# Rows of the scratch list in DRAM: from 1040 bytes to 1088 bytes, and clears in pieces of three rows

## The chip, the cores and the metric

The kernel runs on one core of a Trainium2 chip. The metric is the time of one execution on the device in microseconds (us). Three runs of the kernel before took 1323.39, 1324.07 and 1330.32 us; the median is 1324.07 us. The inputs are four pairs of batches (8 x 1856 tokens of 256 numbers), weights of a spectral layer, and the weights of 16 experts.

## The reference, cut to what matters

Two layers, one behind the other. The first is a transform along the sequence, a complex linear map with a soft threshold, and the transform back:

```
X = rfft(x, axis=1);  Xr, Xi = X.real, X.imag
Yr = Xr @ w_r - Xi @ w_i + b_r;   Yi = Xr @ w_i + Xi @ w_r + b_i
Yr, Yi = soft(Yr, 0.01), soft(Yi, 0.01)          # sign(v) * max(|v| - 0.01, 0)
y = irfft(Yr + 1j * Yi, n=1856, axis=1)
```

The second is a mixture of experts over the 14848 tokens of y. Each token picks one of 4 groups and in it one of 4 experts, by the largest of 4 logits each time:

```
g = argmax(y @ w_group);  e = argmax(y @ w_expert[g])
out = p_g * p_e * (relu(y @ w1[g, e]) @ w2[g, e])  # p_g, p_e: softmax values of the picks
```

## The kernel before, in words

**Stages.** The batches go through in four pairs. For a pair, x is loaded, a short transform (letters a to d of the order below) turns it, 15 steps k do the complex map (e to o), a second transform goes back (p to s) and a third one gives the token rows (t to w), which lie in a tile `vs[pr]` of 128 partitions x 32 rows x 260 numbers (RW = 260: 256 values, the token's number and its gate weight; 1040 bytes). The rows are transposed for the logits (x to z, G, H), and 'R' (route_g, about 30 short VectorE steps for 16 rows) works out to which slot of which expert's list each row goes.

**The list in DRAM.** xs_d has a stretch of CAP rows for each of the 16 experts and 128 rows behind them. Two kinds of work write it. The clears (letter 'Z', line 395, ScalarE's DMA queue, called ACTq in the profile) put zeros into the first NZ = 1152 slots of each expert, 16 transfers and one more (line 393) for the last 128 rows. The scatters ('S', line 272, GpSimd, called POOL) send 128 rows each to their slots by an indirect DMA, 128 scatters in all, 32 for a pair; 12 of each 128 rows have a slot out of bounds and aren't written. They have to come behind the clears. Later the lists are read back: six early blocks of 256 rows (line 777) while the last pairs are still in work, then blocks of 384 or 512 rows (line 430) and 128 or 64 rows (line 1003) for the experts' matmuls, from about 640 us on. The results go to the output by another indirect DMA on GpSimd (line 498).

**What sets the order.** TensorE (PE), ScalarE (ACT) and VectorE (DVE) run the first part in an order written out by hand: the string ORDER, a letter for each step. So a clear is an instruction of ACT that stands between its casts and activations, and what stands behind it on ACT starts when the clear has been issued. The first twelve or so clears stand in the 15 steps k of the first pair. One such step is, on PE, 8 matmuls of line 598 and 24 of line 641; on ACT a cast (607), a negation (611 and 622), two activations (648) and the copy of the bias into the next PSUM tile (627); on DVE lines 616 and 654. POOL and SP (the loads' queue) follow a scheduler. The tiles called `big` rotate through three buffers; a new one waits until the last user of the old one is done.

Of the kernel before, what the change touches and what calls it, by code (L numbers as in the profile page):

```python
# [10 lines left out]
F32 = mybir.dt.float32  # L11
F32R = mybir.dt.float32r
BF16 = mybir.dt.bfloat16
I32 = mybir.dt.int32
# [23 lines left out]
G, EG, NE, F = 4, 4, 16, 1024  # L38
# [3 lines left out]
CAP = N + EARLY  # L42
ROWS = NE * CAP + 128
RW = 260
NZ = 1152
OFF = float(1 << 20)
KF, KH = 7, 4
# [107 lines left out]
def spectral_moe(ctx: ExitStack, tc: tile.TileContext, x, wri, bri, wgate, w1, w2, cst, out):  # L155
    nc = tc.nc

    dram = ctx.enter_context(tc.tile_pool(name="dram", bufs=1, space=bass.MemoryType.DRAM))
    keep = ctx.enter_context(tc.tile_pool(name="keep", bufs=1))
    big = ctx.enter_context(tc.tile_pool(name="big", bufs=3))  # L160
    xp = ctx.enter_context(tc.tile_pool(name="xp", bufs=2))
    ix = ctx.enter_context(tc.tile_pool(name="ix", bufs=1))
    pg = ctx.enter_context(tc.tile_pool(name="pg", bufs=2, space=PSUM))
    xs_d = dram.tile([ROWS, RW], F32, name="xs_d")

    x_v = x.rearrange("pr dc p (r d) -> pr dc p r d", r=32)
    K = keep.tile([128, CK1 - CK0], F32, name="K")
# [11 lines left out]
    for n in (16,):  # L179
        t = keep.tile([128, NE, n], BF16, name=f"smask{n}")  # L180
# [32 lines left out]
    def route_g(pr, L, r0, n):  # L213
# [45 lines left out]
        sloti = rt.tile([128, 16], I32, name="sloti", bufs=3)[:, 0:n]  # L259
        nc.vector.tensor_scalar(out=sloti, in0=slot, scalar1=kc("PO"), scalar2=None, op0=ALU.add)  # L260
        for r in range(n):
            pend.append((pr, sloti[:, r:r + 1], vs[pr][:, r0 + r, :]))
        yield
        nc.vector.tensor_tensor(out=base, in0=base, in1=incf.rearrange("p (e r) -> p e r", e=NE)[:, :, n - 1], op=ALU.add)  # L264
        yield

    pend, sent_of = [], []

    def scatter(n):
        for _ in range(n):  # L270
# [30 lines left out]
    cf = fwd.enter_context(tc.tile_pool(name="cf", bufs=1))  # L301
# [84 lines left out]
    wg = ci.tile([128, 2, 32], F32, name="wg")  # L386
    nc.sync.dma_start(out=wg.rearrange("p c m -> p (c m)"), in_=wgate)
    late.close()
    zero = cf.tile([128, RW], F32, name="zero")
    nc.gpsimd.memset(zero, 0.0)  # L390

    def clear_steps():
        nc.scalar.dma_start(out=xs_d[NE * CAP:ROWS], in_=zero)
        for e in range(NE):
            nc.scalar.dma_start(out=xs_d[e * CAP:e * CAP + NZ].rearrange("(p j) w -> p j w", p=128),
                                in_=zero.unsqueeze(1).broadcast_to([128, NZ // 128, RW]))
            yield

    def raw_w(e):
# [26 lines left out]

    def fetch(pool, e, s0, n, bufs, idb):
        w = n // 128
        xg = pool.tile([128, 4, RW], F32, name="xg", bufs=bufs)
        nc.sync.dma_start(out=xg[:, 0:w], in_=xs_d[e * CAP + s0:e * CAP + s0 + n].rearrange("(p c) w -> p c w", p=128))  # L430
        return xg, ids_of(pool, xg, w, idb)

# [93 lines left out]
    wts, raws, low, units, vs, psum = {}, {}, {}, {}, {}, {}  # L526
    yp, early = [], {}
    jobs = EJOBS
# [147 lines left out]
    @steps_of(pairs, u16)  # L676
    def b_turn(pr, j):
        if j == 0:
            vs[pr] = big.tile([128, 32, RW], F32, name="big")
        nc.vector.transpose(out=vs[pr][:, :, j * 16:(j + 1) * 16].rearrange("p r d -> p d r"),  # L680
                            in_=psum.pop(("b", pr, j)).rearrange("p (k d b) -> p d k b", k=16, b=2))

# [89 lines left out]
    @steps_of(range(len(jobs)))  # L772
    def e_fetch(n):
        j, e = jobs[n]
        assert len(sent_of) >= 64 + 32 * j, "an early list is read before it is written"
        xgs[n] = xg = early["mp"].tile([128, 2, RW], F32, name="xg", bufs=len(jobs))
        nc.sync.dma_start(out=xg, in_=xs_d[e * CAP + j * LEV:e * CAP + j * LEV + LEV].rearrange("(p c) w -> p c w", p=128))

    @steps_of(range(len(jobs)))
# [217 lines left out]
    sp = (mybir.EngineType.SP,)  # L997

    def flex_rows(starts, used_k):
        xg = xq.tile([128, 1, RW], F32, name="xf", bufs=2)  # L1000
        n = 128 // len(starts)
        for i, st in enumerate(starts):
            nc.sync.dma_start(out=xg[i * n:i * n + n, 0, :], in_=xs_d[bass.ds(st, n), :])
        return xg, used_k
# [18 lines left out]

    def flex_ids(rows):
        xg, used_k = rows
        xi = xg[:, 0, :].bitcast(I32)
        nc.vector.tensor_tensor(out=xi, in0=xi, in1=used_k.broadcast_to([128, RW]), op=ALU.bitwise_and)
        return xg, ids_of(xq, xg, 1, 4)

# [174 lines left out]
```

## Time and profile before

| What | Value |
|---|---|
| Median of three runs | 1324.07 us |
| Profiled execution: its time, and its span | 1327.12 us, 1325.3 us |
| PE busy | 1215.2 us, 92% of the span |
| DVE, ACT, POOL busy | 764.1, 696.8, 253.2 us |
| Clears on ACTq: packets of that queue, MB | 19120, 19.46 |
| Scatters and output rows on POOL's queue: packets, MB | 12048, 30.67 |

How to read it: the span is from the first to the last instruction, 1.8 us less than the execution's time. Busy time is a sum over the span; whether an engine limits a stretch is read from that stretch. "issue" behind an idle time means that nothing the profile shows ended it. Issuing a DMA isn't counted as busy for ACT, but nothing behind it on ACT is dispatched before it is issued.

### The profile page before, as it was taken

The page shows a single profiled execution, that of the slowest core. Times are in us where ns is not written, and L with a number is a line of the kernel's source. Part 1 is how long each engine was busy: PE and PEld are TensorE (multiplying, and loading weights), DVE is VectorE, ACT ScalarE, POOL GpSimd, SP SyncE. Part 2 cuts the span into 40 slices and gives each one's busy share as a digit, 9 for nine tenths or more (in the row PEclk, how much of TensorE's full clock was granted, in tenths as well). Part 3 has the DMA queues.
Part 4 walks back from the last instruction along what each step waited for, and adds up shares of the span by engine and source line. Part 5 has one row for each costly group of instructions (what it writes and reads, how often), then busy time and mean ns, then how long its engine had stood idle before and what let it go on. Part 6 is the DMA issues. An engine that isn't in the chain of part 4 may idle for free.

```text
span 1325.3 us, 20451 instructions
## 1 busy us (share of the span) xinstructions
PE 1215.2 (92%) x7418; PEld 1048.9 (79%) x7418; DVE 764.1 (58%) x1706; ACT 696.8 (53%) x1564; POOL 253.2 (19%) x257
## 2 busy tenths in 40 slices
PE   9989997799569977777899999999999999999997
PEld 5978996787369846676798898798798878878886
DVE  5448865288646886644556556455547447446542
ACT  3776894579346745513245445444446345445532
POOL 0000004400440036443101111121121111111111
PEclk9999998799889997977999999999999999999999
DMA  9894103100410013414114345245344434434100
GB/s 383 211 271 105 65 12 112 59 1 33 154 56 4 18 41 121 152 60 153 41 60 151 120 146 207 100 135 220 99 141 155 182 111 155 181 105 159 49 21 29
DMA packets 50198, 151.71 MB, mean 114 GB/s; under 512 B 7205, under 2 KB 27818, under 8 KB 40112
## 3 DMA queue, kind: packets, MB, share of 16 engines
q1 hardware_dynamic: 18928, 100.25, 21.7%
q0 software_dynamic: 12048, 30.67, 6.4%
q10 hardware_dynamic: 19120, 19.46, 5.9%
q8 instruction: 59, 0.97, 0.3%
q14 instruction: 43, 0.35, 0.1%
HBM read 100.40 MB, written 52.46 MB: 115 GB/s over the span
## 4 chain that ended last, share of the span: by engine, by line
PE 79%; DVE 6%; ACT 5%; issue 4%; another core or an unknown queue 3%; ACTq 1%; DMA 1%; POOL 0%; POOLq 0%; DVEq 0%
PE ph L457 21%; PE py L511 15%; PE pw L641 10%; PE py L512 8%; PE bank L314 6%; PE pg L598 3%; PE ph L810 2%; PE bank L711 2%; PE pg L441 2%; PE ph L476 1%; PE bank L831 1%; PE bank L734 1%; PE py L1060 1%; PE ph L1043 1%
## 5 line engine op out<-in xcount | busy, mean ns | idle before, releaser
L511 PE MATMUL py<-big,hh 128*128 128x512 f32 x856 | 309.6, 401 | 0.0
L457 PE MATMUL ph<-xth,big 128*128 128x384 f32 (+1 forms) x928 | 269.0, 365 | 1.7 <-DVE yo L844 1.1
L512 PE MATMUL py<-big,hl 128*128 128x256 f32 x856 | 241.2, 282 | 0.9 <-DVE hl L463 0.9
L498 POOL DMA_INDIRECT out_dram<-yo,si x123 | 119.8, 974 | 617.8 <-DVE yo L519 539.0
L272 POOL DMA_INDIRECT xs_d<-big,sloti x128 | 130.6, 1020 | 428.7 <-DVE base L264 181.7
L463 DVE SCALAR_TENSOR_TENSOR hl<-ph,hh 128x256 fp32r<-128x256 f32 x464 | 157.2, 380 | 77.1 <-ACT hh L461 71.5
L511 PEld LDWEIGHTS py<-big,hh 128*128 128x128 f32 x856 | 161.0, 188 | 38.2 <-issue 3.2
L457 PEld LDWEIGHTS ph<-xth,big 128*128 128x128 f32 x928 | 172.7, 189 | 23.3 <-issue 1.7
L461 ACT ACTIVATE hh<-ph 128x256 fp32r<-128x256 f32 x464 | 139.1, 352 | 84.0 <-PE ph L457 80.6
L518 ACT ACTIVATE yo<-py,gate 128x256 f32<-128x256 f32 x107 | 50.7, 474 | 225.6 <-PE py L512 225.6
L457 PE MATMUL ph<-xtl,big 128*128 128x384 f32 (+1 forms) x464 | 169.2, 365 | 0.0
L512 PEld LDWEIGHTS py<-big,hl 128*128 128x128 f32 x856 | 161.0, 188 | 1.4 <-DVE hl L463 1.2
L519 DVE SCALAR_TENSOR_TENSOR yo<-py,gate,yo 128x256 f32<-128x256 f32 x107 | 51.8, 484 | 183.7 <-ACT yo L518 183.7
L641 PE MATMUL pw<-wh,xh 128*128 128x256 f32 x480 | 123.5, 295 | 1.1 <-ACT xh L611 0.8
L641 PE MATMUL pw<-wl,xh 128*128 128x256 f32 x480 | 120.4, 289 | 0.8 <-issue 0.8
L417 DVE TENSOR_TENSOR big<-xt,big 128x512 fp32r<-128x512 f32 x160 | 108.7, 679 | 0.0
L598 PE MATMUL pg<-CF,big 128*128 128x128 f32 x480 | 73.5, 299 | 32.5 <-issue 23.3
L416 ACT CAST big<-xt 128x512 fp32r<-128x512 f32 x160 | 99.6, 623 | 0.0
L598 PEld LDWEIGHTS pg<-CF,big 128*128 128x128 f32 x480 | 67.0, 209 | 40.8 <-issue 25.4
L641 PEld LDWEIGHTS pw<-wh,xh 128*128 128x128 f32 x480 | 95.1, 198 | 2.6 <-ACT xh L611 1.0
L641 PEld LDWEIGHTS pw<-wl,xh 128*128 128x128 f32 x480 | 95.1, 198 | 2.2 <-issue 1.5
L548 DVE TENSOR_TENSOR sl<-big,sh 128x512 fp32r<-128x512 f32 x128 | 83.7, 684 | 22.6 <-ACT sh L544 20.4
(208 smaller groups left out, 2054.4 us busy)
## 6 DMA issues: line engine op xcount, KB each, us to landing
xt<-in_w_dram SPq DMA_DIRECT2D x46, 1024.0 KB
xs_d<-zero ACTq DMA_DIRECT2D x16, 1170.0 KB
big<-in_w_dram SPq DMA_DIRECT2D x16, 1024.0 KB
big<-in_x_dram SPq DMA_DIRECT2D x8, 1024.0 KB
xt<-in_x_dram SPq DMA_DIRECT2D x8, 1024.0 KB
xg<-xs_d SPq DMA_DIRECT2D x13, 520.0 KB
xg<-xs_d SPq DMA_DIRECT2D x16, 390.0 KB
xs_d<-big,sloti POOLq DMA_INDIRECT x128
```

The costliest lines, as they stand in the source:

```text
L272: ins = nc.gpsimd.indirect_dma_start(out=xs_d, out_offset=bass.IndirectOffsetOnAxis(ap=sl_, axis=0), in_=row, in_offset=None, bounds_check ...
L416: nc.scalar.copy(out=wt[:, 2 * i, cs], in_=raws[i][:, cs])
L417: nc.vector.tensor_tensor(out=wt[:, 2 * i + 1, cs], in0=raws[i][:, cs], in1=wt[:, 2 * i, cs].bitcast(F32), op=ALU.subtract)
L457: nc.tensor.matmul(o[:, :n], lhsT=a_[:, ch, fs], rhs=b_[:, ch, 0:n], start=k == 0, stop=k == 5)
L461: nc.scalar.activation(out=hh[:, f, :m], in_=ov, func=AF.Relu)
L463: nc.vector.scalar_tensor_tensor(out=hl[:, f, :m], in0=ov, scalar=0.0, in1=hh[:, f, :m].bitcast(F32), op0=ALU.max, op1=ALU.subtract)
L498: ins = nc.gpsimd.indirect_dma_start(out=out, out_offset=bass.IndirectOffsetOnAxis(ap=ids.si[:, t:t + 1], axis=0), in_=ysb, in_offset=None ...
L511: nc.tensor.matmul(o, lhsT=hh[:, f, ts], rhs=w2b[:, :, f, :], start=f == 0, stop=f == 7, skip_group_check=True)
L512: nc.tensor.matmul(o[:, 0:D], lhsT=hl[:, f, ts], rhs=w2h[:, f, :], start=False, stop=f == 7, skip_group_check=True)
L548: nc.vector.tensor_tensor(out=lo, in0=src, in1=units[key].bitcast(F32), op=ALU.subtract)
L598: nc.tensor.matmul(o[:, m * 128:(m + 1) * 128], lhsT=zys[pr][:, k, ch * 128:(ch + 1) * 128, bt], rhs=T_v[:, k, :], start=True, stop=True)
L641: nc.tensor.matmul(y[:, bt * D:(bt + 1) * D], lhsT=a_[:, bt * 2 + ch, cs], rhs=w_[:, ri, ch, :], start=False, stop=fin, skip_group_check=True)
```

## The change

Rows of xs_d are 272 numbers apart and long (RP = 272, 1088 bytes) in DRAM and in the tiles into which they are read; in the tile that the scatters read, rows stay 260 numbers apart. A scatter now sends 272 numbers from the row's start, so the last 12 are the first 12 of the next row. Behind row 31 there are 12 new numbers, set to zero by a small memset on GpSimd for each pair. The zero tile is three rows wide, and a clear writes 384 pieces of three rows (3264 bytes) in place of 1152 rows of 1040.

```
+RP = 272
-    xs_d = dram.tile([ROWS, RW], F32, name="xs_d")
+    xs_d = dram.tile([ROWS, RP], F32, name="xs_d")
...
         for r in range(n):
-            pend.append((pr, sloti[:, r:r + 1], vs[pr][:, r0 + r, :]))
+            c = (r0 + r) * RW
+            pend.append((pr, sloti[:, r:r + 1], rows_of_pair[pr][:, c:c + RP]))
...
-    zero = cf.tile([128, RW], F32, name="zero")
+    zero = cf.tile([128, 3, RP], F32, name="zero")
     nc.gpsimd.memset(zero, 0.0)
...
-        nc.scalar.dma_start(out=xs_d[NE * CAP:ROWS], in_=zero)
+        nc.scalar.dma_start(out=xs_d[NE * CAP:ROWS], in_=zero[:, 0])
         for e in range(NE):
-            nc.scalar.dma_start(out=xs_d[e * CAP:e * CAP + NZ].rearrange("(p j) w -> p j w", p=128),
-                                in_=zero.unsqueeze(1).broadcast_to([128, NZ // 128, RW]))
+            nc.scalar.dma_start(out=xs_d[e * CAP:e * CAP + NZ].rearrange("(p a j) w -> p a (j w)", p=128, j=3),
+                                in_=zero.rearrange("p j w -> p (j w)").unsqueeze(1).broadcast_to([128, NZ // 384, 3 * RP]))
...
         if j == 0:
-            vs[pr] = big.tile([128, 32, RW], F32, name="big")
+            rows_of_pair[pr] = t = big.tile([128, 32 * RW + RP - RW], F32, name="big")
+            nc.gpsimd.memset(t[:, 32 * RW:], 0.0)
+            vs[pr] = t[:, 0:32 * RW].rearrange("p (r w) -> p r w", w=RW)
...
-        xgs[n] = xg = early["mp"].tile([128, 2, RW], F32, name="xg", bufs=len(jobs))
+        xgs[n] = xg = early["mp"].tile([128, 2, RP], F32, name="xg", bufs=len(jobs))
```

The tiles of lines 429 and 1000 grow from RW to RP in the same way, and line 1026 masks the first RW numbers of a row only.

On ACT, in the steps k of the first pair, the order of the program before has the first clears here:

```order
L393 DMA xs_d<-zero 128x260 [waits Pool_49]
L395 DMA xs_d<-zero 1152x1x260 x2
L648 ACTIVATE rp<-pw,nlam,CF 128x512 [waits PE_49]
L607 CAST xh<-pg 128x4x128
L611 ACTIVATE xh<-pg 128x4x64
L648 ACTIVATE rn<-pw,nlam,CF 128x512
L622 ACTIVATE xl<-xl 128x4x64 [waits DVE_49]
L627 COPY pw<-bias 128x512 [waits Activation_49]
L395 DMA xs_d<-zero 1152x1x260 [waits DMAHW6_49]
```

and now, two source lines further down:

```order
L395 DMA xs_d<-zero 128x272 [waits Pool_49]
L397 DMA xs_d<-zero 384x1x816 x2
L650 ACTIVATE rp<-pw,nlam,CF 128x512 [waits PE_49]
L609 CAST xh<-pg 128x4x128
L613 ACTIVATE xh<-pg 128x4x64
L650 ACTIVATE rn<-pw,nlam,CF 128x512
L624 ACTIVATE xl<-xl 128x4x64 [waits DVE_49]
L629 COPY pw<-bias 128x512 [waits Activation_49]
L397 DMA xs_d<-zero 384x1x816 [waits DMAHW6_49]
```

Nothing moved: the same 17 transfers stand at the same places behind the same waits, with 384 rows of 816 numbers where there were 1152 of 260.

On POOL, where the scatters of the second pair (big_2916) end and those of the third (big_4317) begin, the order of the program before is

```order
L272 DMA xs_d_72<-big_2916,sloti_4035 245888x260 [waits DMASW6_49,Activation_49]
L272 DMA xs_d_72<-big_2916,sloti_4035 245888x260 [waits DMASW7_49]
L272 DMA xs_d_72<-big_4317,sloti_5129 245888x260 [waits DMAHW4_49,DMASW0_49,DMAHW5_49,DVE_49,Activation_49]
L272 DMA xs_d_72<-big_4317,sloti_5129 245888x260 [waits DMASW1_49]
```

and now (big_2917, big_4319 and big_4918 are the rows of the second, third and fourth pair)

```order
L274 DMA xs_d_72<-big_2917,sloti_4037 245888x272 [waits DMASW6_49]
L274 DMA xs_d_72<-big_2917,sloti_4037 245888x272 [waits DMASW7_49,Pool_49]
L682 MEMSET big_4319 128x12 [waits DMASW4_49,DMASW3_49,DMASW5_49,DMASW2_49,DMASW6_49,DMASW1_49,DMASW7_49,DMASW0_49,PE_49]
L682 MEMSET big_4918 128x12 [waits DVE_49]
L274 DMA xs_d_72<-big_4319,sloti_5133 245888x272 [waits DMAHW4_49,DMAHW5_49,DVE_49,Activation_49]
L274 DMA xs_d_72<-big_4319,sloti_5133 245888x272 [waits Activation_49]
```

Two memsets stand between the scatters of the two pairs: that of the third pair, which waits for all scatters of the second to land, and that of the fourth, which waits for VectorE.

## Rows read from the trace of the kernel before

**Rows 1.** The page: busy time, TensorE's granted clock in 40 slices, the chain by engine.
```profile
PE 1215.2 (92%) x7418; PEld 1048.9 (79%) x7418; DVE 764.1 (58%) x1706; ACT 696.8 (53%) x1564; POOL 253.2 (19%) x257
...
PEclk9999998799889997977999999999999999999999
...
PE 79%; DVE 6%; ACT 5%; issue 4%; another core or an unknown queue 3%; ACTq 1%; DMA 1%; POOL 0%; POOLq 0%; DVEq 0%
```
**Rows 2.** Windows: from:to, length, busy time of each engine, granted clock, DMA.
```profile
core 0: us, PE busy (x) PEld busy (x) DVE busy (x) ACT busy (x) POOL busy (x), PEclk, DMA share, GB/s
...
40.00:49.00 9.00, 9.00 (x80) 9.00 (x79) 3.08 (x5) 6.97 (x15) 0.00 (x0) 1.00 0.96 250
...
60.00:70.00 10.00, 8.00 (x65) 7.50 (x64) 3.42 (x5) 6.30 (x13) 0.00 (x0) 1.00 1.09 271
...
90.00:100.00 10.00, 7.47 (x39) 5.07 (x38) 7.84 (x13) 7.73 (x14) 0.00 (x0) 1.00 1.11 256
100.00:107.00 7.00, 4.67 (x19) 3.27 (x18) 4.35 (x9) 2.66 (x5) 0.00 (x0) 0.90 1.09 283
107.00:130.00 23.00, 23.00 (x160) 21.54 (x159) 21.82 (x31) 16.76 (x34) 0.00 (x0) 0.96 0.24 62
...
160.00:202.00 42.00, 41.83 (x366) 38.50 (x366) 30.43 (x65) 37.28 (x76) 0.00 (x0) 1.00 0.08 26
...
640.00:1325.00 685.00, 670.50 (x3701) 579.74 (x3700) 364.39 (x961) 321.73 (x839) 109.14 (x113) 0.99 0.36 124
```
**Rows 3.** Windows: the sum over six windows that cover 49 to 107 us.
```profile
sum 58.00, PE 49.03 PEld 43.35 DVE 26.36 ACT 37.65 POOL 0.00; mean PE 8.17 PEld 7.23 DVE 4.39 ACT 6.27 POOL 0.00
```
**Rows 4.** Waits of ACT between 49 and 107 us: us in total, times, longest.
```profile
ACT xl L622 <- issue: 7.8, 6, 2.0
ACT pw L627 <- issue: 7.2, 2, 5.0
```
**Rows 5.** Line 395 (ns min/median/max), and ACT's timeline: start, us, [idle before].
```profile
L395 ACTq DMA_DIRECT2D xs_d<-zero x16: 541/1454/4561, 40.0 to 99.0; - x16
...
54.14 2.95 ACTq L395 DMA_DIRECT2D xs_d<-zero  x1
...
57.13 0.42 ACT L622 ACTIVATE xl<-xl 128x256 fp32r<-128x256 f32 x1 [1.75 <-issue]
```
**Rows 6.** The chain between 36 and 110 us: start, us, what.
```profile
38.13 2.83 PE pw L641 x24
...
45.58 2.83 PE pw L641 x24
...
57.55 0.67 ACT rp L648
...
71.35 0.67 ACT rp L648
```
**Rows 7.** DMA between 40 and 49 us, the clears' queue: packets, MB, share.
```profile
q10 hardware_dynamic: 2181, 2.24, 94.5%
```
**Rows 8.** Windows: the sum over six windows in which the scatters run.
```profile
sum 217.00, PE 147.93 PEld 121.69 DVE 98.85 ACT 81.04 POOL 135.46; mean PE 24.66 PEld 20.28 DVE 16.48 ACT 13.51 POOL 22.58
```
**Rows 9.** The page: output rows and scatters (busy, mean ns, idle before), and POOL's queue.
```profile
L498 POOL DMA_INDIRECT out_dram<-yo,si x123 | 119.8, 974 | 617.8 <-DVE yo L519 539.0
L272 POOL DMA_INDIRECT xs_d<-big,sloti x128 | 130.6, 1020 | 428.7 <-DVE base L264 181.7
...
q0 software_dynamic: 12048, 30.67, 6.4%
```
**Rows 10.** Timeline of POOL and DVE: the zero tile, the fourth pair's tile, the third pair's scatters.
```profile
0.73 0.32 POOL L390 MEMSET zero<- 128x260 f32 x1 [0.29 <-POOLq L1192]
...
460.98 1.11 DVE L680 STREAM_TRANSPOSE big<-ph 128x512 f32<-128x512 f32 x1 [0.37 <-PE ph L674]
...
482.26 0.97 POOL L272 DMA_INDIRECT xs_d<-big,sloti  x1 [84.45 <-DVE sloti L260]
483.54 0.97 POOL L272 DMA_INDIRECT xs_d<-big,sloti  x1 [0.30 <-issue]
```

More of the change, by code (lines that the diff above doesn't have):

```diff
@@ L265, in route_g @@
         yield
-    pend, sent_of = [], []
+    pend, sent_of, rows_of_pair = [], [], {}
     def scatter(n):
@@ L428, in fetch @@
         w = n // 128
-        xg = pool.tile([128, 4, RW], F32, name="xg", bufs=bufs)
+        xg = pool.tile([128, 4, RP], F32, name="xg", bufs=bufs)
         nc.sync.dma_start(out=xg[:, 0:w], in_=xs_d[e * CAP + s0:e * CAP + s0 + n].rearrange("(p c) w -> p c w", p=128))
@@ L999, in flex_rows @@
     def flex_rows(starts, used_k):
-        xg = xq.tile([128, 1, RW], F32, name="xf", bufs=2)
+        xg = xq.tile([128, 1, RP], F32, name="xf", bufs=2)
         n = 128 // len(starts)
@@ L1025, in flex_ids @@
         xg, used_k = rows
-        xi = xg[:, 0, :].bitcast(I32)
+        xi = xg[:, 0, 0:RW].bitcast(I32)
         nc.vector.tensor_tensor(out=xi, in0=xi, in1=used_k.broadcast_to([128, RW]), op=ALU.bitwise_and)
```

## The prediction

> **What bounds the kernel now.** I read the page first [rows 1]: TensorE is busy 92% of the span, its clock is granted in full nearly everywhere, and 79% of the chain that ended last is PE. So a faster transfer helps only where PE stands still for it. The windows say where PE does [rows 2]. From 640 us to the end it is busy 670.5 of 685 us; between 107 and 202 us it has practically no gap (23.00 of 23.00, 41.83 of 42.00). Two stretches are left. In the six windows in which the scatters run, PE is busy 147.93 of 217 us, 69.1 us idle [rows 8]. And from 49 to 107 us it is busy 49.03 of 58 us, 9.0 us idle [rows 3]; that is where the clears are issued, the first at 40.0 and the last at 99.0 us [rows 5].
>
> I went into the second stretch with the waits of ACT [rows 4]: 15.0 us, in 8 waits, in front of lines 622 and 627, for "issue", which means that no semaphore ended them. The timeline shows what did [rows 5]: at 54.14 us ACT issues a clear, the issue takes 2.95 us, and the activation of line 622, which stands behind it on ACT, starts only at 57.13, after 1.75 us of idleness. The shortest of the 16 issues takes 0.541 us, the median 1.454 and the longest 4.561. The chain confirms that this reaches PE [rows 6]. At 38.13 and 45.58 us two steps k are 7.45 us apart, 3.73 us a step, and PE's matmuls fill it; from 57.55 to 71.35 three steps take 13.8 us, 4.60 us each, and the chain runs through ACT.
>
> Why the later issues are slow can be worked out. By 49 us four clears and the small one have been issued, (4 x 1152 + 128) / 16 + 5 = 301 packets for each of the 16 DMA engines (a packet a row, one more a transfer for the semaphore). The clears' queue has moved 2181 / 16 = 136 of them [rows 7]. So about 165 are waiting per engine (an estimate), and from there on an issue takes as long as it takes to make room. The transfers run at 250 to 283 GB/s meanwhile, 271 in the middle of the stretch [rows 2].
>
> **The change part by part.** The sum is made against the profiled execution, 1327.12 us (span 1325.3); the median of the runs shown is 3.05 us lower, and I take the difference over to it.
>
> *The clears.* A clear has 384 packets in place of 1152: 25 per engine with the semaphore's, where it had 73. Its bytes grow from 1.198 to 1.253 MB. All 17 transfers now come to (16 x 384 + 128) / 16 + 17 = 409 packets per engine. At 271 GB/s [rows 2] a clear takes 4.62 us to move and PE's pace issues one each 3.73 us, so the queue falls behind by 0.9 us a clear, 14 us by the sixteenth. That is three clears, 75 packets, under half of the 165 at which ACT was held up before. So no issue waits for room any more, and each costs about the 0.54 us of the shortest one before (with a third of the packets hardly more). From 40 to 49 us, while the first four clears were issued, PE was busy 9.00 of 9.00 us [rows 2]: an issue of that size is hidden behind PE's step.
>
> What comes back is at most what PE lost. Its idle time is 9.0 us. Its clock was granted at 0.90 between 100 and 107 us and at 0.96 up to 130 us [rows 2], right behind the longest gaps; without them 0.10 x 7 + 0.04 x 23 = 1.6 us come back as well. And the steps k lost more than the idle time shows, since matmuls that follow a wait are drawn longer: the seven steps up to 90 us at 0.87 us each make 6.1 us, where PE's idle time up to 90 us is 9.0 - 2.53 - 2.33 = 4.1 us (all six windows less those from 90 us on), so 2 us more. The upper bound is 12.6 us. The lower bound: behind 90 us ACT and DVE also wait for each other, on other work than the steps; should all the 4.9 us there stay, with the clock, 4.1 us remain. I take 9.5 us, near the upper end, because ACT's longest wait, 5.0 us in front of line 627 [rows 4], is one for an issue. From 107 to 202 us PE has no slack, so the gain is handed on in full to the first scatter, and from there the same chain starts earlier by that much.
>
> *The scatters.* A row of 1088 bytes in place of 1040. POOL takes 1020 ns for a scatter with rows of 1040 bytes and 974 for output rows of 1024 [rows 9], so a few bytes over 1024 cost nothing that matters, and 48 more should cost between nothing and another 46 ns. On the timeline scatters follow each other each 1.28 us [rows 10], which is POOL's own pace. I take 0; 46 ns x 32 on each pair, 1.5 us, is the other end, and only where PE stands still for a burst.
>
> *The memsets.* The zero tile is three times as wide: 0.32 us at 0.73 us [rows 10], now perhaps 1 us; the first clear is issued at 40.0. The four small ones: that of the third pair waits for scatters that POOL has just issued, 80 us before it issues the next. That of the fourth pair stands in front of the third pair's scatters and waits for VectorE to let go of the old buffer. In the trace VectorE writes the fourth pair's rows into that buffer from 460.98 us on, and the first scatter behind the memset starts at 482.26 [rows 10]: 21 us of cover. They cost nothing.
>
> *The reads.* 4.6% more bytes, one piece a partition as before; they are fetched a job ahead of PE. From 640 us on DMA is busy 0.36 of the time [rows 2]. Nothing.
>
> Sum: 1327.1 - 9.5 = 1317.6 us for a profiled execution, 1324.07 - 9.5 = 1314.6 us for the median.
>
> **A rule that speaks against it.** The row shows issues of up to 4.561 us and 15.0 us of ACT waiting behind them [rows 4, 5]. The Trainium skill (DMA: Bandwidth & Descriptors, "Issuing engines are not separate DMA queues") says that a sequencer's time to initiate a DMA is usually small beside the DMA. By that rule nothing would be won by shorter issues; here the trace disagrees once the queue holds much, and agrees at 0.54 us when it does not. It stands below as the third rival.
>
> **The rivals.**
> 1. *The queue holds bytes, not packets.* The 165 packets are 172 KB per engine, 2.2 of the new clears. With 0.9 us of arrears a clear this is reached at about the eleventh clear; the last five then wait some 0.9 us each, 4 us, and the gain falls to 5.5: 1318.6 us. For it: the trace has only one size of packet at a full queue. Against it: longer pieces may move faster than 271 GB/s, and at 336 GB/s (1.253 MB in 3.73 us) no arrears arise.
> 2. *The scatters were slowed by their rows.* PE's 69.1 us of idleness beside them [rows 8] would shrink, say by half: 1314.6 - 34.5 = 1280 us. For it: it is the largest loss outside PE's work, and it begins with the scatters. Against it: POOL issues them at its own pace, and rows of 1024 bytes go at the same rate as rows of 1040: the whole of POOL's queue is 6.4% of the engines' time [rows 9].
> 3. *ACT's waiting is not what holds PE.* Then DVE's and ACT's own chain keeps the 4.60 us step, or ACT waits as long as before for the transfers, which have 4.6% more bytes: 1324 us. Against it: the same chain makes a step in 3.73 us as long as the issues are short [rows 6].
> 4. *Slower: a row of 1088 bytes makes two descriptors.* POOL would need up to half of its 0.97 us more for each scatter, a burst would last 0.5 / 1.28 = 39% longer, and PE's idle time beside the bursts would grow by 0.39 x 69.1 = 27 us: 1341 us. It decides once POOL takes 0.15 us more for a scatter than now (0.15 / 1.28 x 69.1 = 8 us, most of the gain). Against it: the 1040-byte rows are over 1024 bytes already and show no such step.
>
> Beside rival 2 a sentence of the same page of the Trainium skill ("Specifications") stands: below 512 bytes a write is a read, a change and a write. Rows of 1040 and of 1088 bytes are both above it, so by that rule the scatters gain nothing; no run here shows a shorter row.
>
> **How the numbers follow.** The forecast has 0.70, with a range of its own of 1311 to 1321 us (gains of 12.6 to 4.1, and 1.5 for the scatters); rival 1 0.12, rival 2 0.05, rival 3 0.08, rival 4 0.05. A measurement of this kernel can tell about 0.5%, 6.6 us, from no change, so faster means below 1317.4. Of the forecast's 0.70 I give 0.57 to that and 0.13 to gains under 6.6 us; of rival 1 0.02; all of rival 2: 0.64. Within 0.5%: 0.13 + 0.10 + 0.08 = 0.31. Slower: rival 4, 0.05. The range from 1307 to 1325 us holds the forecast and rivals 1 and 3 with some room below for a burst that falls more luckily on PE's work, and leaves out rivals 2 and 4.
>
> **What would show it.** Right: issues of the clears all under 1 us, no wait for "issue" on lines 624 and 629, steps k of 3.7 us throughout, PE busy nearly all of 49 to 97 us, the first scatter at about 193 us in place of 203, and the same six stretches of idleness beside the scatters, moved. Wrong: issues of 2 us and more (rival 1 if only the last ones), PE's idle time beside the scatters below 60 or above 75 us (rivals 2 and 4), or the first scatter early and the last matmul not.

## The result, and the profile after

The changed kernel takes 1307.44 us (median of 4 runs, 1303.73 to 1309.31), beside 1323.73 us of the kernel before (4 runs, 1318.73 to 1330.32): a ratio of 0.987, 95% interval 0.9822 to 0.9919. The forecast was 1314.6 us, its likeliest case 1311 to 1321 and the whole range 1307 to 1325. The sign was right; the gain is 16.3 us where 9.5 were forecast, outside the likeliest case and at the very edge of the range: 0.987 of the 1324.07 us from which the forecast was made is 1306.9 us, just below it.

The page of the changed kernel, the lines that answer to [rows 1]: PE is busy 8.5 us less in all.

```profile
PE 1206.7 (92%) x7418; PEld 1044.6 (80%) x7418; DVE 763.9 (58%) x1706; ACT 695.9 (53%) x1564; POOL 255.4 (20%) x261
...
PEclk9999998899889988888899999999999999999999
...
PE 77%; DVE 7%; issue 7%; ACT 4%; another core or an unknown queue 3%; POOL 2%; DMA 0%; POOLq 0%; DVEq 0%; ACTq 0%
```

Its windows in the clears' stretch, columns as in [rows 2]: PE without a gap up to 90 us, the clock full throughout, and 353 GB/s between 60 and 70 us where it was 271. From 100 to 107 us nothing moves any more, where it was 283 GB/s.

```profile
40.00:49.00 9.00, 9.00 (x79) 9.00 (x79) 3.18 (x5) 7.31 (x15) 0.00 (x0) 1.00 0.91 357
60.00:70.00 10.00, 10.00 (x87) 10.00 (x87) 3.78 (x6) 8.49 (x17) 0.00 (x0) 1.00 0.90 353
90.00:100.00 10.00, 8.40 (x54) 7.27 (x54) 10.00 (x16) 6.12 (x14) 0.11 (x1) 1.00 0.78 306
100.00:107.00 7.00, 7.00 (x53) 6.60 (x53) 6.67 (x10) 5.45 (x11) 0.00 (x0) 1.00 0.00 0
107.00:130.00 23.00, 23.00 (x158) 21.18 (x157) 22.67 (x33) 18.67 (x36) 0.00 (x0) 1.00 0.06 14
```

The sum from 49 to 107 us, in answer to [rows 3]: 1.6 us idle in place of 9.0.

```profile
sum 58.00, PE 56.40 PEld 53.47 DVE 36.77 ACT 45.76 POOL 0.11; mean PE 9.40 PEld 8.91 DVE 6.13 ACT 7.63 POOL 0.02
```

ACT's waits there for "issue" [rows 4] are 0.8 us in place of 15.0, the longest 0.2 us, and none of them in front of line 629:

```profile
ACT xl L624 <- issue: 0.8, 4, 0.2
```

The clears' issues [rows 5]: the longest of 16 takes 0.657 us in place of 4.561, and the last is issued at 90.5 us.

```profile
L397 ACTq DMA_DIRECT2D xs_d<-zero x16: 541/542/657, 40.2 to 90.5; - x16
```

The chain [rows 6] stays on PE, a step each 3.74 to 3.82 us:

```profile
45.72 2.81 PE pw L643 x24
...
49.46 2.81 PE pw L643 x24
...
53.21 2.81 PE pw L643 x24
...
57.03 2.83 PE pw L643 x24
...
60.81 2.80 PE pw L643 x24
```

The clears' queue from 40 to 49 us [rows 7], 1110 packets and 3.19 MB in place of 2181 and 2.24:

```profile
q10 hardware_dynamic: 1110, 3.19, 89.8%
```

The six windows beside the scatters, moved with them [rows 8]: PE idles 65.9 us in place of 69.1.

```profile
sum 217.00, PE 151.13 PEld 125.45 DVE 101.72 ACT 84.01 POOL 135.56; mean PE 25.19 PEld 20.91 DVE 16.95 ACT 14.00 POOL 22.59
```

The scatters themselves and their queue [rows 9]: 1024 ns where there were 1020.

```profile
q0 software_dynamic: 12048, 31.38, 6.7%
...
L500 POOL DMA_INDIRECT out_dram<-yo,si x123 | 120.7, 981 | 615.6 <-DVE yo L521 537.5
...
L274 POOL DMA_INDIRECT xs_d<-big,sloti x128 | 131.0, 1024 | 305.1 <-DVE base L266 137.8
```

Where the time came from is read from POOL's timeline, since both kernels issue the same scatters in the same order. The scatters come in bursts of 16. In the changed kernel the first scatter of all, the first of the fifth burst (the 65th), and the 17th and the 121st output scatter:

```profile
191.48 1.12 POOL L274 DMA_INDIRECT xs_d<-big,sloti  x1 [100.34 <-DVE base L266]
...
465.86 0.97 POOL L274 DMA_INDIRECT xs_d<-big,sloti  x1 [48.62 <-DVE sloti L261]
...
668.03 0.97 POOL L500 DMA_INDIRECT out_dram<-yo,si  x1 [1.80 <-DVE yo L521]
...
1292.32 0.97 POOL L500 DMA_INDIRECT out_dram<-yo,si  x1 [1.81 <-DVE yo L521]
```

In the kernel before (its fifth burst, 482.26 us, is in [rows 10]):

```profile
202.95 1.12 POOL L272 DMA_INDIRECT xs_d<-big,sloti  x1 [181.75 <-DVE base L264]
...
684.63 0.97 POOL L498 DMA_INDIRECT out_dram<-yo,si  x1 [1.85 <-DVE yo L519]
...
1311.46 0.97 POOL L498 DMA_INDIRECT out_dram<-yo,si  x1 [1.86 <-DVE yo L519]
```

Up to the first scatter 11.5 us are gained; from there to the fifth burst (279.31 us before, 274.38 after) 4.9; from the fifth burst to the 17th output scatter 0.2; from there to the 121st (626.83 and 624.29 us) 2.5. With 0.1 behind it that is 19.2 us, the difference of the two spans (1325.3 and 1306.1). The first part is the forecast's step; the 4.9 and the 2.5 us were in no step. The record doesn't say on which chip these first two traces were taken, so they may come from two.

### The profile page after: what moved, and what is told of

Read it like the earlier page. It is cut to its first block, busy times and chain, and to the rows that moved or that the text cites. A ratio compares the mean times of both kernels' runs of the same rounds, so it can differ in the third digit from the quotient of the medians.

```text
span 1306.1 us, 20467 instructions
## 1 busy us (share of the span) xinstructions
PE 1206.7 (92%) x7418; PEld 1044.6 (80%) x7418; DVE 763.9 (58%) x1706; ACT 695.9 (53%) x1564; POOL 255.4 (20%) x261
## 4 chain that ended last, share of the span: by engine, by line
PE 77%; DVE 7%; issue 7%; ACT 4%; another core or an unknown queue 3%; POOL 2%; DMA 0%; POOLq 0%; DVEq 0%; ACTq 0%
PE ph L459 21%; PE py L513 15%; PE pw L643 11%; PE py L514 8%; PE bank L316 6%; PE pg L600 4%; PE pg L443 2%; PE bank L715 2%; PE ph L478 1%; POOL xs_d L274 1%; DVE sl L550 1%; PE py L1064 1%; PE ph L1047 1%; PE bank L738 1%
## 5 line engine op out<-in xcount | busy, mean ns | idle before, releaser
L274 POOL DMA_INDIRECT xs_d<-big,sloti x128 | 131.0, 1024 | 305.1 <-DVE base L266 137.8
L459 PEld LDWEIGHTS ph<-xtl,big 128*128 128x128 f32 x464 | 87.9, 189 | 8.5
```

Of the source, the lines that this page charges most:

```text
L274: ins = nc.gpsimd.indirect_dma_start(out=xs_d, out_offset=bass.IndirectOffsetOnAxis(ap=sl_, axis=0), in_=row, in_offset=None, bounds_check ...
L459: nc.tensor.matmul(o[:, :n], lhsT=a_[:, ch, fs], rhs=b_[:, ch, 0:n], start=k == 0, stop=k == 5)
```

## The experiments

The runs came in six groups, each taken together on one chip ("this call" in the expectations is such a group). They fell on four chips, and these differ: before takes 1247 us on two of them (called quick here) and 1311 to 1318 us on the others. So each time is compared with before's in the same group, and the traces by the same four parts.

**First group, a quick chip.** Three theories for the 4.9 us: rows of 1088 bytes disturb PE less (A); work that is early meets the bursts at a better phase (B, later W); or it is chance and the chip's condition (C, later V). And which half of the change frees ACT? The clears alone, with rows of 1040 bytes:

```
-    zero = cf.tile([128, RW], F32, name="zero")
+    zero = cf.tile([128, 3, RW], F32, name="zero")
...
-  ... rearrange("(p j) w -> p j w", p=128), in_=zero.unsqueeze(1).broadcast_to([128, NZ // 128, RW])
+  ... rearrange("(p a j) w -> p a (j w)", p=128, j=3), in_=zero.rearrange("p j w -> p (j w)")
+                                             .unsqueeze(1).broadcast_to([128, NZ // 384, 3 * RW])
```

> The clears of the change alone: pieces of three rows, while rows stay 1040 bytes (a piece is 3120 bytes) and the scatters and reads are as before. Open is where the 17 us come from: in the traces the first scatter starts 11.5 us earlier than before, and some 5 us more arise beside the third and fourth burst of scatters. All theories: issues of the clears about 0.54 us, the first scatter at about 191.5 us instead of 202.95. Theory A (the bytes and the alignment of the scattered rows give the 5 us): the end is 11 to 12 us earlier than before (ratio 0.991), and PE's busy time beside the fourth burst stays near 11 of 23 us. Theory B (the 5 us come only because everything meets the bursts 11.5 us earlier, a matter of phase): 16 to 17 us earlier (0.987). Theory C (the 5 us are scatter between executions): anything from 9 to 17 us, and PE's idle time beside the bursts varies by some us between profiles of the same kernel.

Measured: ratio 0.9974 (0.9965 to 0.9983); issues of at most 0.654 us, the first scatter at 192.34 us. So larger pieces alone free ACT. The gain at the end is 3 us, and none of the three theories' 9 to 17; their numbers came from traces in which before is 76 us slower.

The rows alone (of the changed kernel, with clears of a row a packet):

```
-    zero = cf.tile([128, 3, RP], F32, name="zero")
+    zero = cf.tile([128, RP], F32, name="zero")
...
+  ... rearrange("(p j) w -> p j w", p=128), in_=zero.unsqueeze(1).broadcast_to([128, NZ // 128, RP])
```

> The 1088-byte rows of the change alone: scatters, reads and memsets as after, but a clear writes 1152 rows of 1088 bytes, a packet each. If packets in the queue are what holds ACT, the issues of the clears are slow again (median over 1.2 us, longest over 3 us) and the steps k 4.6 us, if the aligned rows don't move faster; if alignment to 64 bytes alone lifts the rate from 271 towards 400 GB/s, the arrears vanish and the issues stay near 0.54 us. Theory A (rows give the 5 us beside the scatters): with slow issues 5 us faster than before (ratio 0.996). Theory B (phase): with slow issues within 2 us of before (0.998 to 1.002). Theory C: within 4 us of before.

Measured: ratio 0.9953 (0.994 to 0.9966), the first scatter at 191.99 us. Line 397 and the window from 50 to 90 us:

```profile
L397 ACTq DMA_DIRECT2D xs_d<-zero x16: 541/691/1683, 39.9 to 90.7; - x16
```

```profile
50.00:90.00 40.00, 40.00 (x316) 38.80 (x314) 19.91 (x31) 33.26 (x64) 0.00 (x0) 1.00 1.10 344
```

With as many packets as before the clears move at 344 GB/s, and PE has no gap. So the rows alone are enough too, and it is not the number of packets that held ACT, but the rate at which they leave.

The changed kernel again:

> The changed kernel again, beside the others on one chip. Theories A and B: 16 to 17 us faster than before (ratio 0.987), with the same places of the gain as in its first trace: 11.5 us at the first scatter, about 16 at the fifth burst. Theory C: the gain at the first scatter is again 11.5 us, but what is gained beside the third and fourth burst differs by 3 us or more from the 5 of the first trace, and the total lies between 11 and 19 us.

Measured: 1239.10 us, ratio 0.9931 (0.9918 to 0.9944). The first scatter stands at 191.44 us as in its first trace, but here the stretch to the fifth burst takes 230.17 us and not 274.38, and the gain of 8.9 us is in none of the three theories' ranges: what scatters cost PE differs by chip.

The kernel before, with its clears spread in the order string (a Z after two in three steps k, later one in 28 letters):

```
-...nijoZZemfkghnijoZemfkghnijoZemfkghnijoZemnkfojghZiemnkfojghZ...
+...nijoemfkghnijoZemfkghnijoZemfkghnijoemnkfoZjghiemnkfoZjghi...
```

> The kernel before with nothing changed but where its clears stand on ACT: the 16 clears of 1152 rows of 1040 bytes are issued over some 110 us instead of 59, two in three steps k and then one each 7 us or so, so that the queue moves one (4.4 us at 271 GB/s) before too many wait. If the full queue is what holds ACT: issues under 1 us, steps k of 3.75 us, the first scatter about 11 us earlier, with the old packets. If the packets' number itself costs ACT time (descriptors written at the issue), issues stay at 1.4 us in the median and less than 5 us come back. At the end: theory A about 11 us faster than before (ratio 0.991 to 0.992), theory B 16 to 17 us (0.987), theory C 9 to 17 us.

Measured: ratio 0.9946 (0.9934 to 0.9959); the first scatter at 190.77 us, the earliest of all. Line 395:

```profile
L395 ACTq DMA_DIRECT2D xs_d<-zero x16: 541/542/631, 43.7 to 140.3; - x16
```

The old packets are issued in 0.54 us if the queue has time to move them. So the hold is the queue's arrears, as the forecast had it. At the end 0.9946 is short of what all three theories expected (0.987 to 0.993).

**Second group, the other quick chip.** What was missing is a trace of before from such a chip.

> The kernel before itself, for a trace of it from the chip of the experiments, where it takes 1248 us and not 1324. Theory P (the 75 us between the two chips are PE's idle time beside the scatters, which is then the chip's and not the rows'): up to 200 us the trace is that of before, with issues of the clears of up to 4 us and more and the first scatter at about 203 us; the six stretches beside the scatters lose some 15 us in place of 69; the clear stage is 11 us longer than in the changed kernel, and some 2 to 3 us of it are given back behind it. Theory Q (the clears move faster on that chip, and the gain of 8.9 us is the whole of what the clear stage loses): first scatter at 200 us, issues of up to 2 us. In both the ratio is 1.000.

Measured: ratio 0.9992; line 395 and the window from 50 to 90 us:

```profile
L395 ACTq DMA_DIRECT2D xs_d<-zero x16: 541/1120/4279, 39.9 to 94.4; - x16
```

```profile
50.00:90.00 40.00, 39.05 (x308) 36.91 (x306) 15.99 (x25) 30.09 (x59) 0.00 (x0) 1.00 1.09 297
```

The longest issue is that of theory P. The first scatter comes at 195.96 us, earlier than either theory had it (203 and 200 us), 4.5 behind the changed kernel's, since the old clears move at 297 GB/s here, as in Q. In six windows beside its scatters, 196 us in all, PE idles 23.7 us, nearer to P's 15 than to 69. Of the 79.6 us between the spans of the two traces of before (1325.3 and 1245.7), 48.8 lie between the first scatter and the fifth burst (279.31 and 230.47 us) and 19.7 between that and the last scatter (123.53 and 103.82).

The clears alone again, beside it:

> The clears in pieces of three rows alone, again, beside a trace of before from the same chip. If the chip is like the last one: 3 us faster than before (ratio 0.9975), first scatter at 192.3 us. If scatters cost PE as much as in the first traces: theory A (rows of 1088 bytes disturb PE less) 11 to 12 us faster (0.991); theory B (phase) 16 to 17 us (0.987).

Measured: ratio 0.998 (0.9969 to 0.9991), the first scatter at 192.14 us, as the first time.

Then the packets' starts (the rows alone, with each clear begun 16 bytes further on):

```
-  out=xs_d[e * CAP:e * CAP + NZ].rearrange("(p j) w -> p j w", p=128)
+  out=xs_d.rearrange("r w -> (r w)")[e * CAP * RP + 4:(e * CAP + NZ) * RP + 4]
+        .rearrange("(p j w) -> p j w", p=128, w=RP)
```

> 1088-byte rows as in the run that has them alone (a clear is 1152 packets of 1088 bytes), but each clear begins 16 bytes behind the start of its first slot, so that no packet begins at a multiple of 64 bytes; the first four numbers of an expert's first slot aren't cleared. If it is the packets' starts that brought the rate from 271 to 350 GB/s: back to about 270 to 280 GB/s, issues of up to 4 us and a first scatter at 201 to 204 us (the end 5 to 9 us later than with the rows alone). If it is their length in bytes (1088 against 1040): 350 GB/s, issues of up to 1.7 us, the first scatter at 192 us.

Measured: ratio 1.0175 (1.016 to 1.0191), the first scatter at 219.55 us.

```profile
L397 ACTq DMA_DIRECT2D xs_d<-zero x16: 542/2884/5527, 40.0 to 113.0; - x16
```

```profile
50.00:90.00 40.00, 30.43 (x233) 29.20 (x232) 9.48 (x14) 20.35 (x41) 0.00 (x0) 0.96 1.14 226
```

Sixteen bytes cost a third of the rate (344 to 226 GB/s) and 27.6 us up to the first scatter: the starts decide, more strongly than expected. (They are counted from the start of xs_d; a shift moves a packet's end as well.) Larger pieces hide most of it: in the clears alone three of four pieces of 3120 bytes begin off a multiple of 64, and between 49 and 60 us they move at 394 GB/s, where the changed kernel's 3264 bytes have 402.

To gain by both, the changed kernel with the spread clears:

> The changed kernel with its clears spread over some 100 us as in the run that spread those of before, to beat both. That run reached the first scatter 0.7 us before the changed kernel and the 57th vector step of the maps 1.25 us before it, and lost this again behind 640 us, where kernels with 1040-byte rows take some 2.4 us longer. If the two gains add up: 1.0 to 1.5 us faster than the changed kernel, ratio to before 0.992. If what is left in the clear stage is not issue time: the same as the changed kernel, 0.993.

Measured: 1239.86 us, ratio 0.9937 (0.9923 to 0.995), the first scatter at 191.47 us, the changed kernel's. The 0.7 us by which the spread clears of before came earlier (190.77) weren't added to it, and no version was faster than the changed kernel where both were measured.

**Third group, a chip on which scatters cost much.** In all traces up to here the stretch from the 17th to the 121st output scatter takes 624.29 or 624.30 us with the rows of 1088 bytes and 626.75 to 626.84 with those of 1040. The kernel before with nothing changed but sizes of tiles on the chip:

```
+RP = 272
-        xg = pool.tile([128, 4, RW], F32, name="xg", bufs=bufs)
+        xg = pool.tile([128, 4 * RP], F32, name="xg", bufs=bufs)[:, 0:4 * RW].rearrange("p (c w) -> p c w", w=RW)
```

and the same for the early blocks' xg, for xf and, with 12 numbers more, for big.

> Between 640 us and the end all kernels with 1088-byte rows so far take the same time to 0.05 us, and all with 1040-byte rows take 2.4 us more, spread over the blocks (31.52 us for four output scatters where the others have 31.21). This run has the kernel before with rows of 1040 bytes in DRAM and the same transfers, but the tiles on the chip get the sizes of the changed kernel (4 x 272 numbers a partition for the lists' rows, 12 more for each pair's rows), of which only the old part is used. Theory S (the tiles behind are placed otherwise on the chip, and matmuls read them a little faster): 31.21 us a block and 2.4 us less than before from 640 us on, ratio 0.998. Theory D (the reads of aligned rows from DRAM): 31.52 us as before, ratio 1.000. In both the clears' stage is that of before.

Measured: ratio 0.9982 (0.9967 to 0.9997). POOL's timeline, the 17th and the 121st output scatter, 624.14 us apart:

```profile
667.92 0.97 POOL L499 DMA_INDIRECT out_dram<-yo,si  x1 [1.80 <-DVE yo L520]
...
1292.06 0.97 POOL L499 DMA_INDIRECT out_dram<-yo,si  x1 [1.81 <-DVE yo L520]
```

Theory S: the 2.5 us come from the tiles' sizes, with the old rows in DRAM. The matmuls of the experts' second layer show where. Between the two output scatters (count, busy us, mean ns) this kernel has

```profile
L512 PE MATMUL py<-big,hh 128*128 128x512 f32 x805 | 289.8, 400 | 0.0
L513 PE MATMUL py<-big,hl 128*128 128x256 f32 x804 | 225.4, 280 | 0.0
```

and the one before

```profile
L511 PE MATMUL py<-big,hh 128*128 128x512 f32 x805 | 291.2, 401 | 0.0
L512 PE MATMUL py<-big,hl 128*128 128x256 f32 x804 | 226.3, 282 | 0.0
```

With equal counts the two lines are 1.4 and 0.9 us shorter, most of the 2.7 us between 626.83 and 624.14; the rest lies in lines that differ by 0.3 us or less. Which of the four tiles does it wasn't tried, and why a matmul takes a ns or two less isn't shown.

The clears alone, beside it:

> The clears in pieces of three rows alone, a third time: the chips differ, and on the first one (1324 us before) the changed kernel gained some 5 us more beside the third and fourth burst of scatters, on the later ones under 1. If this chip is like the later ones (before at 1247 us): 3 us faster than before, ratio 0.9975, the first scatter at 192.3 us. If it is like the first one: theory A (rows of 1088 bytes disturb PE less) 11 to 12 us faster, 0.991; theory B (the bursts meet other work because all is 11.5 us earlier) 16 to 17 us, 0.987.

Measured: ratio 0.9983 (0.9965 to 1.0001), neither 0.991 nor 0.987. From the first scatter to the fifth burst it takes 270.37 us and the wide tiles 268.07, both with the old rows; the changed kernel's first trace had 274.38. So old rows can be as quick there as new ones.

**Fourth group, the same chip.** Before and after in one group:

> The kernel before once more, with its own trace beside one of the changed kernel from the same chip. Open is whether the first trace of before (1327 us) is typical: there the clears moved at 271 GB/s (295 in the next trace of before) and PE lost some 5 us more beside the third and fourth burst than with any kernel since, old rows or new. Theory V (both are of that chip or that execution, not of the rows): clears at 285 to 300 GB/s, the first scatter at 196 us, and where the time of before is above 1300 us, its five bursts cost what they cost in the runs with the old rows on such a chip (fifth burst begins 268 us behind the first, not 279). Theory W (a kernel whose first scatter comes late meets the bursts at a worse phase): the later the first scatter, the more is lost; at 203 us the fifth burst begins 279 us behind it, at 196 us 268. Ratio 1.000 in both.

> The changed kernel a third time. From the runs so far its parts are 4.5 to 5 us in the clears' stage where the old clears move at 295 GB/s (11.5 at 271), 2.4 us from 640 us on by the tiles' places on the chip, and nothing beside the scatters. Theory V: 7 to 9 us faster than before (ratio 0.993 to 0.995) where the clears of before move at 295 GB/s, whatever the scatters cost on the chip; 14 us (0.989) where they move at 271. Theory A, left from the first runs (rows of 1088 bytes disturb PE less where scatters cost much): 12 us and more (0.990) at 295 GB/s on a chip where before takes over 1300 us.

Measured: ratio 1.0018 for before itself, 0.9905 (0.9872 to 0.9939) for the changed kernel. First scatters at 197.44 and 191.30 us, the clears of before at 286 GB/s; to the fifth burst 276.03 and 270.82 us. The first scatter is near V's, but that before takes 276 and not 268 us to the fifth burst is neither V's nor W's number, and 0.9905 is A's. So A, W and V had to be told apart in one group.

**Fifth and sixth group.** The half-shifted kernel has the new rows but comes late; the clears alone have the old rows and come early:

```
+    def off(e):
+        return 4 if e < 8 else 0
...
+  out=xs_d.rearrange("r w -> (r w)")[e * CAP * RP + off(e):(e * CAP + NZ) * RP + off(e)]
```

> New rows, late: 1088-byte rows, a packet a row in the clears, and the first eight clears begin 16 bytes behind their slot's start, which slows them (225 GB/s where all sixteen were shifted). The first four numbers of eight experts' first slots aren't cleared. All theories: the first scatter at 202 to 206 us, as late as in the first trace of before or later. From the first scatter to the fifth burst, on a chip where before takes over 1300 us: theory A (rows of 1088 bytes disturb PE less) as in the changed kernel of this call to 2 us, the end 11 to 14 us later than that kernel's; theory W (late kernels meet the bursts at a worse phase) 5 us longer than the changed kernel, like before's, the end 16 to 20 us later. On a chip where before takes 1247 us the stretch is 230 to 231 us for all, and nothing is told apart.

> Old rows, early: the clears in pieces of three rows alone. First scatter at 192.3 us. From the first scatter to the fifth burst, on a chip where before takes over 1300 us: theory A as in before of this call, so that the end is 8 to 9 us behind the changed kernel's (5 for the bursts, 2.4 from 640 us on, 0.9 in the clears); theory W as in the changed kernel, the end 3 to 4 us behind it. Theory V: 268 to 279 us, without order among the four kernels. On a chip where before takes 1247 us: 4.5 us behind the changed kernel, as it was there.

> The kernel before, for its trace in this call. First scatter at 196 to 203 us by the rate of its clears (295 to 271 GB/s). From there to the fifth burst, on a chip where it takes over 1300 us: theories A and W 5 us longer than in the changed kernel of this call; theory V shorter or longer.

> The changed kernel, for its trace in this call. First scatter at 191.4 us as in all its traces. From there to the fifth burst 270 to 275 us on a chip where before takes over 1300 us, 230 us where it takes 1247. Ratio to before: 0.987 to 0.991 on the former (theories A and W), 0.993 on the latter; theory V: 0.987 to 0.996 on the former.

Measured, on a quick chip: ratios 1.007 (1.0053 to 1.0088), 0.9983 (0.9972 to 0.9994), 1.0007 and 0.994 (0.9923 to 0.9957). All four take 229.5 to 230.5 us to the fifth burst, which tells nothing apart but gives a third pair of before and after. So the two were run once more, and fell on a chip where before takes 1316 us:

> New rows, late, once more (the first four numbers of eight experts' first slots aren't cleared). First scatter at 206 to 209 us. On a chip where before takes over 1300 us, from the first scatter to the fifth burst: theory A 271 to 274 us and less than in the run with old rows beside it; theory W 276 to 279 us and 5 us more than there. Theory V: the two runs of this call within 3 us of each other, whatever their rows and their start. On a chip where before takes 1247 us: 230 us, ratio 1.007, nothing told apart.

> Old rows, early, once more: clears in pieces of three rows alone. First scatter at 192.3 us. On a chip where before takes over 1300 us, from the first scatter to the fifth burst: theory A 276 to 279 us; theory W 270 to 274 us; theory V within 3 us of the run with the new rows beside it. On a chip where before takes 1247 us: 230 us, ratio 0.998.

Measured: ratios 1.0034 (1.0015 to 1.0053) and 0.9981 (0.9958 to 1.0005). The first scatter and the fifth burst of the half-shifted kernel, 273.35 us apart:

```profile
206.47 1.12 POOL L274 DMA_INDIRECT xs_d<-big,sloti  x1 [100.62 <-ACT pw L632]
...
479.82 0.97 POOL L274 DMA_INDIRECT xs_d<-big,sloti  x1 [48.78 <-DVE sloti L261]
```

and of the clears alone, 273.08 us apart:

```profile
191.98 1.12 POOL L272 DMA_INDIRECT xs_d<-big,sloti  x1 [170.89 <-DVE base L264]
...
465.06 0.97 POOL L272 DMA_INDIRECT xs_d<-big,sloti  x1 [81.21 <-DVE sloti L260]
```

They are 0.3 us apart, where A wanted about 5 in one direction and W about 5 in the other. But the fifth burst isn't the last. The 17th output scatter of the half-shifted kernel and that of the clears alone:

```profile
677.37 0.97 POOL L503 DMA_INDIRECT out_dram<-yo,si  x1 [1.80 <-DVE yo L524]
```

```profile
670.22 0.97 POOL L498 DMA_INDIRECT out_dram<-yo,si  x1 [1.81 <-DVE yo L519]
```

From the first scatter to there the late kernel with new rows takes 470.90 us and the early one with old rows 478.24, 7.3 more. The other two pairs of new and old rows have the same sign: 476.55 and 481.68 us in the first traces of after and before, 475.75 and 479.09 in the fourth group. The medians agree in part: of the 14.5 us between the first scatters the tiles' 2.5 come off, so 12.0 are due at the end if neither theory holds, and with the 5 us of the first traces taken off 7 by A, put on 17 by W (an estimate); 8.9 are measured (1321.91 and 1313.05 us), uncertain by about 4 after the two intervals. So W alone is out as far as one pair tells; A, neither, and both together are left. Against A stand the third group's old rows with 471.32 us (wide tiles) and 474.01 (clears alone), and the half-shifted kernel's traced execution was the fastest of its twelve.

Three pairs of before and after (the second and third of one group each), gain in us by part:

| Part | first traces | group 4 | group 5, quick chip |
|---|---|---|---|
| up to the first scatter | 11.5 | 6.1 | 4.4 |
| to the fifth burst | 4.9 | 5.2 | -0.1 |
| to the 17th output scatter | 0.2 | -1.9 | 0.1 |
| to the 121st, and behind it | 2.6 | 2.8 | 2.7 |
| span | 19.2 | 12.3 | 7.1 |
| difference of the medians | 16.3 | 10.9 | 8.1 |

## Why the prediction was wrong, point by point

**Which step failed: the sum.** It gave the whole gain to the clears, 9.5 us, and put the reads and the scatters at nothing. In the first traces 11.5 us came from the clears; 2.5 from the tile sizes, on the lines of "The reads. Nothing."; and 4.9 beside the scatters, "I take 0", whose cause stays open. The mechanism of the clears was right, its size too small.

**ACT is held by the queue, and PE by ACT: right.** Three edits that have nothing in common but that the queue keeps up (larger pieces, aligned rows, the same clears spread out) bring the first scatter to 190.8 to 192.3 us, and slower packets bring it to 219.6. The signs named beforehand came: issues under 1 us, steps of 3.7 to 3.8 us, PE busy up to 90 us, the first scatter at 191.5 where 193 was forecast; only line 624 kept four waits for an issue, 0.8 us in all. The third rival falls. The Trainium skill (DMA: Bandwidth & Descriptors, "Issuing engines are not separate DMA queues") calls the time to initiate a DMA usually small beside the DMA: 0.54 us in the spread run agrees, up to 5.53 us in the shifted run, where a clear takes 5.55 us to move, does not.

**The size of that term: too small, and taken from the wrong row.** Forecast 9.5 us, measured 11.5. PE's idle time shows a loss only in part: in [rows 2] a matmul is drawn with 8.00 / 65 = 0.123 us between 60 and 70 us, where it has 9.00 / 80 = 0.113 before 49. The arithmetic that the prediction used for the new clears gives the old ones better: a clear leaves in 1.198 MB / rate, PE issues one each 3.73 us, and the sixteen differences add up to the delay. Set against the first scatter's delay behind the changed kernel's 191.48 us:

| Kernel | GB/s, 50 to 90 us | 16 x (time to move a clear - 3.73) | measured delay |
|---|---|---|---|
| shifted (1.253 MB) | 226 | 29.0 | 28.1 |
| before, first trace | 274 | 10.3 | 11.5 |
| before, group 4 | 286 | 7.3 | 6.0 |
| before with wide tiles | 293 | 5.7 | 5.1 |
| before, group 2 | 297 | 4.9 | 4.5 |
| before, group 5 | 297 | 4.9 | 4.3 |
| rows alone (1.253 MB) | 344 | none | 0.5 |

So the term is 4.3 to 11.5 us according to the rate that an execution gives the old rows. The column is a fit to these rows and not the mechanism in full: it leaves out the packets that the queue holds before ACT is held up, and that the changed kernel's 16 issues, 40.2 to 90.5 us, lie 3.35 us apart. In the changed kernel it is gone: its first scatter stands between 191.30 and 191.48 us in all four traces.

**"At 271 GB/s a clear takes 4.62 us to move": wrong, without harm.** The new clears move at up to 402 GB/s (49 to 60 us). The prediction kept the old rate for want of another row; its result, no hold, was the same. The first rival's slow last issues don't come, since no arrears arise; whether the queue's room is counted in packets or in bytes is therefore not tested.

**"The reads. Nothing.": wrong by 2.5 us.** The bytes themselves cost nothing that shows (624.14 us with the old rows in wide tiles, 624.29 with the new rows), but the step spoke only of them. The same lines make tiles on the chip larger, and matmuls of the main stage get a ns or two shorter. The run with nothing but wide tiles shows it. It lies in all kernels with the sizes of the changed one, to 0.2 us, and in none without.

**"The scatters. I take 0.": right for POOL, open for PE.** POOL's 1024 ns for a scatter exclude the fourth rival, and the second rival's halved idle time (69.1 to 34.5 us) didn't come: 65.9 us. The 5 us up to the fifth burst stand in two pairs of traces where scatters cost much. Up to there the rows don't sort the runs (old rows took 268.1, 270.4, 273.1, and in before 276.0 and 279.3 us, new ones 270.8, 273.4 and 274.4), nor does lateness (206.47 us with 273.35, 191.98 with 273.08). Read to the 17th output scatter, though, the new rows are 3.3 to 7.3 us shorter in each of the three pairs, and the medians leave about 2 us for this part and the ones around it (16.3 - 11.5 - 2.5 and 10.9 - 6.1 - 2.5), inside the intervals. Executions of one sort of rows differ by as much (471 to 482 us with old ones). So the rows or chance: that stays open.

**The chances.** The bounds of the first term (4.1 to 12.6 us) held it on each chip. What was missing was width for terms set at nothing, and the sense that "before" itself can be the unsteady one of the two: in group 4 its 18 runs span 1311 to 1327 us, the 7 of the changed kernel 1303.5 to 1308.1.

## What to carry to other kernels

Where an engine that computes also issues transfers, compare the time in which one moves with the time between two issues; the difference, added up, is what the issuing engine loses, and it can be mended by faster packets, larger ones, or later issues. Where rows of about 1 KB are written to DRAM a packet each, try starts at multiples of 64 bytes, and measure it: here 16 bytes cost a third of the rate (other offsets, 32 bytes say, weren't tried by themselves). An edit that alters a tile's size can shift the durations of instructions far away by a ns or two, presumably by moving tiles on the chip (not shown): compare lines over the same work, not only the step that was edited.

## What the hardware showed that was not expected

Writes of 1088 bytes a packet from the same tile moved at 344 GB/s when they began at multiples of 64 bytes in DRAM and at 226 when they began 16 bytes behind. The Trainium skill (DMA: Bandwidth & Descriptors, "How a descriptor splits into AXI transactions") says of reads that 32-byte beats count from the 256-byte boundary below a start. Were it the same for writes, the shift would add about one beat to 37, an estimate of 3%, so that rule doesn't account for the third that was measured. What does stays open.

One program takes 1247 us on two chips and 1311 to 1324 on the others. The mean granted clock is 0.98 on the former and 0.96 on the latter; by an estimate that is 0.02 of PE's 1215 us, 24 of some 70. From the first scatter to the fifth burst it takes 230 us on the former and 268 to 279 on the latter, while POOL takes the same time for a scatter. The traces show in what form PE loses it: between 190 and 680 us its waits for "issue", which nothing that the profile shows ends, are 32.7 to 43.0 us in each of the eight traces in which it is slow, and 0 in all twelve from the quick chips. What causes them was not found.
